# Row sums of a batch's first chunk in 64x32 tiles by query halves, and stages in a new order, in a fused attention and MoE kernel

## The chip, the cores and the metric

The kernel runs on one core of a Trainium2 chip. The metric is the time of one execution on the device, in microseconds (us). A core has five engines that run side by side, each through its own instructions in order: TensorE (PE, matrix products, with its weight loads shown apart as PEld), VectorE (DVE), ScalarE (ACT), GpSimd (POOL) and SyncE (SP, which here only issues transfers). Transfers (DMAs) run on 16 DMA engines, fed by the queues of SP, ACT and POOL.

## The reference

Eight batches of twelve heads, 448 positions, head size 64, all fp32:

```python
q_n, k_n = rmsnorm(q, g_q), rmsnorm(k, g_k)
scores = (q_n @ k_n.T) / sqrt(64)
attn = exp(scores - max) / sum(exp(scores - max))
x = (attn @ v), heads side by side        # 3584 tokens x 768
h = x @ w_in                              # 768 -> 2048
g = h + sin(alpha * h)**2 / alpha
out = g @ w_out                           # 2048 -> 768, fp32
```

## The kernel before

**Tiling.** A batch is a stage. Its twelve heads form three chunks (c = 0, 1, 2) of four heads: two heads `pp` lie on partition halves, two heads `hi` beside each other. Scores are computed transposed, with 64 keys on the partitions and 448 queries along the free dimension: `scores` makes one such tile (four 64x64 matmuls into a pair of PSUM banks), and ScalarE's exp (L361) writes it to SBUF as bf16. There are 7 tiles of keys a chunk, 21 a batch. `attend` then accumulates, over the 7 tiles, the values (weights from `vb`) and the sums of the exponentials over the keys (weights are a tile of ones, so that each sum appears on as many PSUM partitions as the weights have columns). ScalarE turns sums into reciprocals as exp(-ln(sum)) (L412, L413); VectorE multiplies the values by them into `xT` (L421), the input of the first product.

Chunk 0 is treated alone ("ones 0", "values 0"), with 64x64 tiles: contraction over 64 keys (row half `pp`), output on the 64 partitions of `hi`, in the bank `pp`. Chunks 1 and 2 go together ("ones 1", "low 1", "high 1") in 64x32 tiles, eight at a time.

**The two products.** `first_product` computes h in 16 blocks of 128 features, 8 pairs of banks, six 128x128 matmuls a block (L449). Its first four blocks take the k tiles in the order 0, 1, 2, 4, 3, 5, all four blocks at each; tiles 0 and 1 come from chunk 0 and use the first 256 rows of `w_in` (pieces W00, W10), tiles 2 and 3 use W01 and W11, 4 and 5 W02 and W12 (first digit: half of the features; second: rows). ScalarE's sine (L427), a square on GpSimd or ScalarE (L430, L432) and VectorE (L435) make g. `second_product` cuts the output into units of 128 tokens by 384 columns, with 64x64 tiles (L528); VectorE copies and adds the two halves (L534, L535) into one of three `osb` buffers, and SP stores it. The last batch's second product uses whole 128x128 tiles (L509).

**Order.** Each engine's order is written out by hand in the strings `STAGE_0` (batch 0), `STAGE_1` (batch 1) and `STAGE_N` (batches 2 to 7). Tokens are read from left to right: `S` a score tile (`S2` with two matmuls on zeros ahead of it), `o`, `v`, `x`, `y`, `z` with a number so many key tiles of ones 0, values 0, ones 1, low 1, high 1; a number n is n steps of the second product of the batch before (eight matmuls each) and `f` a step of the unit after the current one; `q`, `u`, `g`, `r`, `k` are squares, their reduction, the scaling by g, the inverse root and the scaling of a chunk of q and k; `p` transposes a chunk on PE, `t` by DMA; `l` loads a chunk, `V` values, `W` and `O` pieces of `w_in` and `w_out`; `D` is a small GpSimd copy that waits until a chunk has landed, so that loads behind it start later. A dictionary gives tokens that come at points of the first product. The second string of a stage lists which of four PSUM bank pairs each allocation takes, in order. An allocation waits until the readers of the pair before it have finished. The load of a chunk (three `qk` buffers) waits until its buffer has been read.

The changed lines stand in `attend`, in the plan strings and in the call that loads chunk 1.

Of the kernel before, what the change touches and what calls it, by code (L numbers as in the profile page):

```python
# [17 lines left out]
try:  # L18
# [8 lines left out]
ACT = mybir.ActivationFunctionType  # L27
# [3 lines left out]

STAGE_0 = (
    (
        "q000 u000 G q010 q011 u010 q001 u011 r01 u001 r00 g00 q11 q10 g01 k01 D1 k00 V00 L p012 p00 u10 "
        "V01 u11 W12 S2 S q20 r1 u20 g1 k11 l3 q21 k10 S2 l4 S S4 S W01 g2 S1 u21 p1 r2 k20 o7 S1 V02 S "
        "q30 k21 v7 u30 S S4 q31 D2 u31 S S1 W00 p2 r3 S3 g3 S S2 k31 S2 q40 D4 W02 S2 k30 q41 p3 S1 u40 "
        "W10 l5 W11 O01 q51 S x4 u41 y3 q50 S r4 z2 z2 x3 y4 g4 z1 z2 "
    ),
    "30123103213013230120310232103102310231302130213",
    {-1: 'u50 u51 g5', 1: 'k401 O00 l6', 2: 'k411', 3: 'O10', 4: 'k400', 5: 'k410', 7: 'O11', 8: 'p4 V12 l7 V10 V11'},  # L40
)
STAGE_1 = (
    (
        "2 q31 4 q40 S 2 u31 S 1 S 1 S r2 1 f q41 1 f 1 S S 1 f f k21 k20 1 S t2 2 S 2 S 1 u40 u41 1 q30 "
        "g3 S 2 f o2 u30 S r4 f 1 f 1 S 1 f o5 2 f r3 l5 2 f g4 f S 2 S 2 V11 S 1 S 2 k31 v1 k41 k30 k40 "
        "S v2 S v4 V12 S y1 S y1 S z3 x7 z3 q51 y5 l6 V10 z1 "
    ),
    "0212310313131230222101013032013001230123",
    {-1: 'l7 q50', 0: 'u51', 2: 'g5 t4', 4: 'u50', 8: 't3'},
)  # L50
STAGE_N = (
    (
        "1 r2 q31 q30 f 2 S V10 f 3 V11 f f k20 2 S 3 S 2 k21 S u31 q40 1 t2 1 g3 1 S 1 f u30 S 2 f S f S "
        "r3 q41 f f 1 l5 1 f S 4 u40 S S 5 S S u41 o7 v7 S S 5 S 2 q51 f S 2 S q50 k31 k30 2 S g4 1 u50 S "
        "2 r4 t3 1 S z3 x7 k40 y7 z1 z2 z1 "
    ),
    "01232302102020301301320321310130210231023",
    {-1: 'l6 u51 V12', 1: 'k41', 2: 't4 l7', 3: 'g5'},
)
LAST = "0123012"  # L60

# [7 lines left out]
def kernel(  # L69
# [23 lines left out]
    nc = tc.nc  # L93
    B, H, S, D = q.shape
# [8 lines left out]
    NJ = S // REST  # L103
    assert P == 2 * REST == 2 * D
    NC = NP // 2
# [28 lines left out]
    def bank_pair(name, dtype=F32):  # L134
        slot = int(upcoming.popleft())
        free_at.remove(slot)
        ps = psum.tile([P, 2, 2048 // mybir.dt.size(dtype)], dtype, tag=f"ps{slot}", name=name)
        slot_of[id(ps)] = slot
        return ps

    def give_back(ps):
        free_at.append(slot_of.pop(id(ps)))
# [3 lines left out]
    def strip(c, pp, hi):  # L146

        s = 2 * hi + (pp if c == 1 else 1 - pp)
        return slice(s * 32, s * 32 + 32)

    def load_qk(ci, k_queue=nc.sync):

        b, dp = ci // NC, ci % NC
        qk[ci] = inp.tile([P, 2, 2 * NJ, D], F32, tag="qk", name="qk")
        for which, src, queue in ((0, q, nc.sync), (1, k, k_queue)):
            heads = src[b].rearrange("(dp hi pp) (p j) d -> dp pp p hi (j d)", hi=2, pp=2, j=NJ)[dp]
            rows = qk[ci][:, which].rearrange("p (hi j) d -> p hi (j d)", hi=2)
            if ci == 0:
                continue
            if dp < 2:  # L160
                queue.dma_start(out=rows, in_=heads.rearrange("pp p hi x -> (pp p) hi x"))
            else:
                for pp in range(2):
                    queue.dma_start(out=rows[pp * 64:pp * 64 + 64], in_=heads[1 - pp])
        if ci == 0:
            for hi in range(2):
                for which, src, queue in ((0, q, nc.sync), (1, k, k_queue)):
                    heads = src[b].rearrange("(dp hi pp) (p j) d -> dp hi pp p (j d)", hi=2, pp=2, j=NJ)[dp, hi]
                    rows = qk[ci][:, which].rearrange("p (hi j) d -> p hi (j d)", hi=2)
                    queue.dma_start(out=rows[:, hi], in_=heads.rearrange("pp p x -> (pp p) x"))  # L170
                if hi == 0:
                    load_g()
# [17 lines left out]
    def load_g():  # L190
        for i, (src, queue) in enumerate(((g_q, nc.sync), (g_k, nc.scalar))):
            queue.dma_start(out=g_rows[:, i], in_=src.rearrange("(a d) -> a d", a=1))

    load_qk(0, nc.scalar)
    load_qk(1, nc.scalar)
    load_qk(2)
    nc.gpsimd.dma_start(out=small, in_=moe_alpha.rearrange("(mt p) -> mt p", p=P))
    nc.scalar.preload_act_table_set(EXP_LN)
# [2 lines left out]
    ones = const.tile([P, D], BF16)  # L201
# [58 lines left out]
    qkT, expT, xT = {}, {}, {}  # L260
# [125 lines left out]
    def attend(b, what, tiles=range(NJ)):  # L386

        kind, both = what.split()  # L390
        both = both == "1"
        if tiles[0] == 0:
            avs[what] = bank_pair("av")
        av = avs[what]
        pre = presums.get(b) if what == "ones 0" else None
        last = 1 if pre else NJ - 1
        for j in tiles:
            for hi in range(2):
                for c in ((1, 2) if both else (0,)):
                    for pp in range(2):  # L400
                        r = slice(pp * 64, pp * 64 + 64)
                        o, k = (strip(c, pp, hi), c - 1) if both else (slice(hi * 64, hi * 64 + 64), pp)
                        d = slice(kind == "high", D, 2) if both and kind != "ones" else slice(D // 2 if both else D)
                        w = ones[r, d] if kind == "ones" else vb[b][r, 2 * c + hi, j, d]
                        x = pre.parts[j] if pre else expT[b * NC + c, j]
                        nc.tensor.matmul(av[o, k, :S], w, x[r, hi, :], start=(j == 0), stop=(j == last))  # L406
        if tiles[-1] < last:
            return
        if kind == "ones":
            rec = recs[both] = pre.t if pre else rpool.tile([P, 2, S], F32, tag="rec", name="rec")  # L410
            for k in ((0, 1), (1, 2)) if both and b == 0 else ((0, 2),):
                nc.scalar.activation(rec[:, slice(*k)], av[:, slice(*k), :S], ACT.Ln)  # L412
                nc.scalar.activation(rec[:, slice(*k)], rec[:, slice(*k)], ACT.Exp, scale=-1.0)  # L413
            give_back(avs.pop(what))
        else:
            if b not in xT:
                xT[b] = xpool.tile([P, KT, S], BF16, tag="xT", name="xT")
            first = 0 if not both else 2 if kind == "low" else 3
            for k in (slice(0, 1), slice(1, 2)) if both and b == 0 else (slice(0, 2),):
                kts = slice(first + k.start * (1 + both), first + (k.stop - 1) * (1 + both) + 1, 1 + both)  # L420
                nc.vector.tensor_mul(xT[b][:, kts, :], av[:, k, :S], recs[both][:, k])  # L421
            give_back(avs.pop(what))
# [185 lines left out]
    for b in range(B):  # L608
        plan, slots, h_plan = (STAGE_0, STAGE_1, STAGE_N)[min(b, 2)]
        if b:  # L610
            nc.scalar.preload_act_table_set(EXP_LN)
            fillers.extendleft(reversed(second_product(b - 1)))
        tiles = deque((b * NC + c, j) for c in range(NC) for j in range(NJ))
        upcoming.extend(slots)
        done = {what: 0 for what in STEPS}
        for x in tokens_of(plan):
            if x in "Ff":
                fill(x == "f")
            elif x[0] == "S":
                scores(*tiles.popleft(), int(x[1:] or 0))  # L620
            elif x[0] in STEPS:
                n = int(x[1:] or 1)
                attend(b, STEPS[x[0]], range(done[x[0]], done[x[0]] + n))
                done[x[0]] += n
            else:
                step(b, x)
        first_product(b, {i: [lambda t=t: step(b, t) for t in tasks.split()] for i, tasks in h_plan.items()})
        assert not upcoming and not tiles
# [32 lines left out]
```

## Time and profile before

The median of three runs is 416.54 us (416.4 to 418.31). The profiled execution took 419.68 us, of which the profile's span is 417.9 us.

| engine | busy us | share of the span |
|---|---|---|
| PE | 397.1 | 95% |
| ACT | 317.4 | 76% |
| POOL | 285.3 | 68% |
| DVE | 227.1 | 54% |

"Busy" is the time in which an engine had at least one instruction at work; matmuls overlap on PE, so a busy PE needn't be at its peak. A group of instructions is named by its line, its engine and its operands as out<-in. The chain of waits follows the last instruction back to what released each step, and so shows which engine or transfer sets the end. `x` and a number count instructions. Lines of DMA in it give the start and the time from issue to landing.

### The profile page before, as it was taken

The numbers are of one execution on the slowest core, as the hardware profiler recorded it, in microseconds if no ns is written. First come the engines' busy times: TensorE is split into PE (matmuls) and PEld (weight loads), VectorE is DVE, ScalarE is ACT, GpSimd is POOL, SyncE is SP. The second block draws the span as 40 slices with busy tenths as digits, with TensorE's granted clock in tenths as the row PEclk, the third lists the DMA queues.
The fourth block names the chain that finished last, engine by engine and source line by source line (L and its number), as shares of the span: only waits on it lengthen the run. The fifth ranks groups of instructions, "written<-read, shape, count | busy, mean of one in ns | idle before, by whom it ended". The sixth has DMA issues, their size and how long they took to land.

```text
span 417.9 us, 14897 instructions
## 1 busy us (share of the span) xinstructions
PE 397.1 (95%) x6598; PEld 238.2 (57%) x6601; DVE 227.1 (54%) x339; ACT 317.4 (76%) x467; POOL 285.3 (68%) x270
## 2 busy tenths in 40 slices
PE   2797999889999999999999999999999999999996
PEld 2243558645666557655666456655576556665563
DVE  5786475426674565564575466655565464335511
ACT  4897789748889679877889688987889688886600
POOL 4999889966786879597796688597795784003300
PEclk9999999999999999999999999999999999999999
DMA  8999999798085744847374744736385521620022
GB/s 244 212 220 255 167 218 156 168 284 105 3 164 131 168 139 83 175 92 156 101 175 119 174 134 80 176 81 164 104 131 158 93 46 27 96 61 0 2 75 75
DMA packets 66788, 54.51 MB, mean 130 GB/s; under 512 B 38164, under 2 KB 62500, under 8 KB 66724
## 3 DMA queue, kind: packets, MB, share of 16 engines
q1 hardware_dynamic: 53250, 40.06, 37.8%
q0 software_dynamic: 12512, 11.81, 19.7%
q10 hardware_dynamic: 962, 1.70, 1.1%
q8 instruction: 51, 0.84, 0.8%
q14 instruction: 13, 0.11, 0.1%
HBM read 45.62 MB, written 11.01 MB: 136 GB/s over the span
## 4 chain that ended last, share of the span: by engine, by line
PE 86%; DMA 6%; POOL 4%; issue 2%; DVE 1%; ACTq 0%; SPq 0%; ACT 0%; DVEq 0%; POOLq 0%
PE hps L449 34%; PE ops L528 29%; PE av L406 11%; PE sc L358 6%; PE ops L509 5%; DMA w_in<-in_moe_w_in_dram 3%; DMA qk<-in_k_dram 2%; POOL sq L283 1%; DMA out_dram<-osb 1%; POOL qk L288 1%; POOL vb L182 0%; POOL vb L185 0%; SPq L499 0%; POOL w_in L244 0%; DVE osb L534 0%
## 5 line engine op out<-in xcount | busy, mean ns | idle before, releaser
L361 ACT ACTIVATE expT<-sc 128x896 bf16<-128x896 f32 x168 | 144.9, 914 | 16.9 <-PE sc L358 16.0
L449 PE MATMUL hps<-xT,w_in 128*128 128x448 bf16 x768 | 146.8, 353 | 2.1 <-DMA w_in<-in_moe_w_in_dram 2.1
L528 PE MATMUL ops<-w_out_sb,g_sb 64*64 64x384 bf16 x3072 | 145.6, 323 | 0.2 <-ACT expT L361 0.2
L435 DVE SCALAR_TENSOR_TENSOR g_sb<-s,inv_alpha_sb,hps 128x448 bf16<-128x448 f32 x128 | 80.8, 677 | 67.3 <-POOL s L430 66.9
L449 PEld LDWEIGHTS <-w_in 128*128 128x128 bf16 x768 | 74.4, 98 | 74.0 <-issue 3.0
L528 PEld LDWEIGHTS <-g_sb 64*64 64x64 bf16 x3072 | 91.3, 107 | 38.0 <-issue 2.7
L430 POOL TENSOR_TENSOR s<-s 128x448 f32<-128x448 f32 x64 | 59.5, 932 | 74.7 <-ACT s L427 50.2
L427 ACT ACTIVATE s<-hps,alpha_sb 128x448 f32<-128x448 f32 x128 | 74.4, 626 | 43.2 <-PE hps L449 40.4
L283 POOL TENSOR_TENSOR sq<-qk 128x896 f32<-128x896 f32 x44 | 73.3, 1682 | 26.1 <-DMA qk<-in_k_dram 21.1
L311 POOL TENSOR_TENSOR qkn<-qk,inv 128x448 bf16<-128x448 f32 x80 | 72.7, 938 | 2.5 <-ACT inv L302 2.0
L358 PE MATMUL sc<-qkT 64*64 64x448 bf16 x672 | 58.3, 356 | 3.6 <-DVE qkT L343 2.1
L534 DVE COPY osb<-ops 128x384 f32<-128x384 f32 x48 | 26.7, 557 | 51.3 <-PE ops L528 46.1
L288 POOL TENSOR_TENSOR qk<-qk,gg 128x896 f32<-128x896 f32 (+1 forms) x25 | 50.3, 2016 | 1.2 <-ACT g_sb L280 1.1
L292 DVE TENSOR_REDUCE ms<-sq 128x14 f32<-128x896 f32 x44 | 46.7, 1078 | 6.4 <-POOL sq L283 6.3
L421 DVE TENSOR_TENSOR xT<-av,rec 128x896 bf16<-128x896 f32 (+1 forms) x26 | 25.6, 1015 | 37.2 <-ACT rec L413 30.7
L406 PE MATMUL av<-expT,vb 64*32 64x448 bf16 (+1 forms) x1120 | 37.9, 350 | 2.7 <-issue 2.0
L432 ACT ACTIVATE s<-s 128x448 f32<-128x448 f32 x64 | 36.9, 577 | 3.0 <-DVE g_sb L435 0.2
L358 PEld LDWEIGHTS <-qkT 64*64 64x64 bf16 x672 | 20.7, 107 | 17.3 <-issue 7.9
L406 PEld LDWEIGHTS <-vb 64*32 64x32 bf16 (+1 forms) x1120 | 19.5, 95 | 16.7 <-issue 6.8
L535 DVE TENSOR_TENSOR osb<-osb,ops 128x384 f32<-128x384 f32 x48 | 26.6, 554 | 1.7
L406 PE MATMUL av<-expT,ones 64*32 64x448 bf16 (+1 forms) x672 | 24.5, 349 | 0.0
L509 PE MATMUL ops<-w_out_sb,g_sb 128*128 128x384 bf16 x128 | 21.0, 326 | 0.0
(46 smaller groups left out, 173.5 us busy)
## 6 DMA issues: line engine op xcount, KB each, us to landing
out_dram<-osb SPq DMA_DIRECT2D x39, 192.0 KB, 3.7
qk<-in_q_dram SPq DMA_DIRECT2D x15, 448.0 KB, 5.5
qk<-in_k_dram SPq DMA_DIRECT2D x14, 448.0 KB, 6.3
qk<-in_q_dram SPq DMA_DIRECT2D x18, 224.0 KB, 4.3
qk<-in_k_dram SPq DMA_DIRECT2D x16, 224.0 KB, 4.7
vb<-in_v_dram POOLq DMA_DIRECT2D x16, 224.0 KB, 4.4
w_out_sb<-in_moe_w_out_dram POOLq DMA_DIRECT2D x4, 768.0 KB, 7.7
out_dram<-osb SPq DMA_DIRECT2D x26, 96.0 KB, 3.4
```

The costliest lines, as they stand in the source:

```text
L283: nc.gpsimd.tensor_mul(st.sq[w], qk[ci][:, w], qk[ci][:, w])
L288: nc.gpsimd.tensor_mul(x, x, gg.to_broadcast([P, len(heads) * NJ, D]))
L292: nc.vector.reduce_sum(st.ms[:, w, rows], st.sq[w][:, rows], axis=AX.X)
L311: eng.tensor_mul(n[:, :, hi, :], x[:, hi], inv[:, hi].unsqueeze(2).to_broadcast([P, NJ, D]))
L358: nc.tensor.matmul(sc[pp * 64:pp * 64 + 64, hi, :S], qkt[r, 1, j * REST:(j + 1) * REST], qkt[r, 0, :], start=True, stop=True)
L361: nc.scalar.activation(expT[c, j], sc[:, :, :S], ACT.Exp, scale=SCALE)
L406: nc.tensor.matmul(av[o, k, :S], w, x[r, hi, :], start=(j == 0), stop=(j == last))
L427: nc.scalar.activation(s1, hps, ACT.Sin, scale=alpha_sb[:, m, :])
L430: nc.gpsimd.tensor_mul(s2, s1, s1)
L435: nc.vector.scalar_tensor_tensor(g_sb[:, m, (b % 2) * S:(b % 2 + 1) * S], s2, inv_alpha_sb[:, m, :], hps, op0=ALU.mult, op1=ALU.add)
L449: nc.tensor.matmul(ps[:, m % 2, :S], w_in_sb[m * 2 // MT][:, kt, m % (MT // 2) * P:(m % (MT // 2) + 1) * P], x[:, kt, :], start=(kt == ORD ...
L528: nc.tensor.matmul(st["ps"][os, r, :HALF], g_sb[rs, m, c0 + o * 64:c0 + o * 64 + 64], w_out_sb[rs, m, half * HALF:(half + 1) * HALF], star ...
```

## The change

In batches 1 to 7 the sums of chunk 0 are made in 64x32 tiles: each of the four (pp, hi) sums is split into the two halves `qh` of the queries, and each half gets its own strip of 32 PSUM partitions, so that eight matmuls of 224 columns take the place of four of 448. A strip then holds the sums of one half of the queries only. ScalarE makes the reciprocals of both strips in three instructions (one Ln, two Exp, 448 elements each), and four VectorE copies bring each half's reciprocals to the other strip of its pair, so that the multiply finds them on all 64 partitions. Batch 0 keeps the sums as they were.

All three plans are new: the order of tokens, the bank pairs and the tokens beside the first product. Chunk 1's k is loaded from SP's queue and not from ACT's.

```diff
     load_qk(0, nc.scalar)
-    load_qk(1, nc.scalar)
+    load_qk(1)
     load_qk(2)
...
         last = 1 if pre else NJ - 1
+        halved = what == "ones 0" and b > 0
         for j in tiles:
+            if halved:
+                for hi in range(2):
+                    for qh in range(2):
+                        for pp in range(2):
+                            r, o = slice(pp * 64, pp * 64 + 64), slice((2 * hi + qh) * 32, (2 * hi + qh) * 32 + 32)
+                            nc.tensor.matmul(av[o, pp, :S // 2], ones[r, :D // 2], expT[b * NC, j][r, hi, qh * S // 2:(qh + 1) * S // 2],
+                                             start=(j == 0), stop=(j == NJ - 1))
+                continue
...
             rec = recs[both] = pre.t if pre else rpool.tile([P, 2, S], F32, tag="rec", name="rec")
-            for k in ((0, 1), (1, 2)) if both and b == 0 else ((0, 2),):
+            if halved:
+                cols = [slice(0, S // 2), slice(S // 2, S)]
+                nc.scalar.activation(rec[:, :, cols[0]], av[:, :, cols[0]], ACT.Ln)
+                nc.scalar.activation(rec[:, :, cols[1]], rec[:, :, cols[0]], ACT.Exp, scale=-1.0)
+                nc.scalar.activation(rec[:, :, cols[0]], rec[:, :, cols[0]], ACT.Exp, scale=-1.0)
+                for hi in range(2):
+                    for qh in range(2):
+                        src, dst = (slice((2 * hi + x) * 32, (2 * hi + x) * 32 + 32) for x in (qh, 1 - qh))
+                        nc.vector.tensor_copy(rec[dst, :, cols[qh]], rec[src, :, cols[qh]])
+            for k in () if halved else ((0, 1), (1, 2)) if both and b == 0 else ((0, 2),):
                 nc.scalar.activation(rec[:, slice(*k)], av[:, slice(*k), :S], ACT.Ln)
                 nc.scalar.activation(rec[:, slice(*k)], rec[:, slice(*k)], ACT.Exp, scale=-1.0)
```

The plans, cut to what the prediction speaks of:

```diff
 STAGE_0 = (
     (
-        "... D1 k00 V00 L p012 p00 u10 V01 u11 W12 S2 ... W01 g2 ... V02 ... D2 ... W00 ... D4 W02 ... W10 l5 W11 O01 ..."
+        "... D1 k01 k00 V02 W00 p012 q11 g1 W02 ... q21 ... q20 ... V00 g2 ... W11 q30 ... q31 ... V01 S D2 g3 k31 W01 l5 o3 W10 o3 D4 W12 ..."
...
 STAGE_1 = (
     (
-        "2 q31 4 q40 S ... k21 k20 1 S t2 2 S ... o2 ... o5 ... v1 ... v2 S v4 V12 S y1 S y1 S z3 x7 z3 q51 y5 l6 V10 z1 "
+        "1 q31 2 S 2 q30 ... k20 f k21 f S t2 f 1 S ... u40 o6 V12 o1 v1 2 S 2 f r3 v4 S v2 1 k31 f S f S 1 S f 1 S 1 k30 1 t3 S q50 2 S S z4 l6 S r4 x5 x1 z1 x1 y6 V11 y1 z1 z1 g5 k41 k40 "
...
 STAGE_N = (
     (
-        "1 r2 q31 q30 f 2 S V10 ... S S 5 S S u41 o7 v7 S S 5 S 2 ... 2 r4 t3 1 S z3 x7 k40 y7 z1 z2 z1 "
+        "f q40 f 1 f 2 q41 1 S 1 r2 5 f S f f S 2 S 1 u40 k20 1 k21 S 1 u41 1 S 2 S 1 q31 1 o7 1 f f 1 S t2 f 1 r4 S 2 f 1 l5 q30 S 3 S 1 u31 1 S 2 u30 g3 V10 S 2 S S k41 3 S v6 r3 k30 S k31 v1 S 2 V12 g4 2 S 2 S 2 q51 l6 S t3 z3 x7 y5 y2 z4 V11 "
-    "01232302102020301301320321310130210231023",
+    "01223131310312323203013012301021310231023",
-    {-1: 'l6 u51 V12', 1: 'k41', 2: 't4 l7', 3: 'g5'},
+    {-1: 'k40', 0: 't4', 2: 'q50', 3: 'u50', 4: 'u51 g5', 6: 'l7'},
```

## The prediction

> **What bounds the kernel.** I read the page's busy shares first (PE 95%), then busy time in windows cut where each batch's first product starts and, for the first three, ends.
>
> ```profile
> core 0: us, PE busy (x) PEld busy (x) DVE busy (x) ACT busy (x) POOL busy (x), PEclk, DMA share, GB/s
> 0.00:41.79 41.79, 28.99 (x459) 13.83 (x462) 29.62 (x51) 30.87 (x48) 34.86 (x41) 1.00 1.01 233
> ...
> 57.85:90.20 32.35, 28.76 (x721) 21.34 (x722) 14.92 (x24) 27.44 (x36) 31.01 (x30) 1.00 0.88 194
> ...
> 137.50:184.81 47.31, 47.31 (x855) 28.83 (x854) 27.09 (x40) 39.07 (x58) 37.35 (x34) 1.00 0.58 136
> ```
>
> A steady stage (47.31 us) is all PE: 47.31 busy, at full clock, with the others at 39, 37 and 27. Stage 1's attention (57.85 to 90.20) has 3.6 us without PE. Stage 0 is bound elsewhere: DMA is at its limit (share 1.01), and the chain of waits runs through one weight load:
>
> ```profile
> 30.60 11.14 DMA w_in<-in_moe_w_in_dram
> 41.74 0.05 issue
> 41.79 16.06 PE hps L449 x84
> ```
>
> PE had started that product at 37.20, did 12 matmuls and stood 2.1 us. The waits inside 57.85 to 90.20 name stage 1's loss:
>
> ```profile
> DVE osb L534 <- DMA out_dram<-osb: 5.1, 2, 3.9
> ...
> PE av L406 <- issue: 1.6, 1, 1.6
> ...
> PE sc L358 <- DVE osb L535: 1.4, 1, 1.4
> ...
> PE av L406 <- DVE osb L535: 0.4, 1, 0.4
> ```
>
> Stores stand on SP's queue behind a transpose that waits for GpSimd; VectorE's copies wait for the stores' buffers (three), and PE twice for a bank (1.8 us). The 1.6 us has no visible cause.
>
> Last, PE in order of time in a steady stage:
>
> ```profile
> 171.18 1.49 PE L406 MATMUL av<-expT,ones 64*64 64x448 bf16 x28
> 172.51 1.49 PE L406 MATMUL av<-expT,vb 64*64 64x448 bf16 x28
> ...
> 180.36 0.36 PE L358 MATMUL sc<-qkT 64*64 64x448 bf16 x4
> 180.65 0.76 PE L406 MATMUL av<-expT,vb 64*32 64x448 bf16 x24
> 181.22 1.51 PE L406 MATMUL av<-expT,ones 64*32 64x448 bf16 x56
> 182.55 2.27 PE L406 MATMUL av<-expT,vb 64*32 64x448 bf16 x88
> 184.75 18.33 PE L449 MATMUL hps<-xT,w_in 128*128 128x448 bf16 x96
> ```
>
> Seven groups of four 64x64 matmuls take 1.33 us (171.18 to 172.51); so do seven groups of eight 64x32 matmuls (181.22 to 182.55). Both are 0.19 us a group: eight run side by side as readily as four, and columns set the time. From 180.36 to 180.65 one group costs 0.29: a change of tile shape adds 0.10.
>
> [...]single records here start 3 to 4 ns apart, eight within 24. [...]
>
> **The change, part by part.** *Sums.* Per batch, 7 groups of four 448-column matmuls become 7 groups of eight of 224: 7 x (0.189 - (224/2.4 + 2.3 = 0.0957)) = 0.65 us less on PE. The 28 added matmuls, each with its weight load, are inside that figure if loads keep up[...]. I take 0.096, since 64x32 loads start 3 to 4 ns apart in the trace and none delays a group.
>
> *Tile changes.* The sums used to sit between 64x64 work. Now they are entered and left once in stages 2 to 7: +0.10 + 0.12 = 0.22 us. Counting changes along the plans, stage 1 has seven before and seven after (it loses two detours at its end), so 0.
>
> *ScalarE.* Before 0.92 + 0.95 = 1.87 us (Ln, Exp, 896 elements). After Ln 0.534 and two Exp of 0.577, the 448-element rows of batch 0: 1.69. It has 8 us of slack a stage: 0.
>
> *Copies.* Four per stage, fp32, SBUF to SBUF, 448 elements, 32 partitions; no row before shows one. [...]So 1.6 to 2.5 us a stage, on an engine idle for 20. What can suffer is what queues behind them. Running sum of a steady stage from its start (a fill of eight matmuls 0.325, a score group 0.19, an exp 0.83 to 0.91, first exp at 3.1 behind the table load as before): seventh score at 9.0, its exp ends at 10.4, the sums reach their seventh group at 10.55 (0.15 to spare) and end at 10.65. Ln and Exps fill 10.9 to 12.6, copies 12.6 to 14.2. The unit of the second product that ends at 14.4 needs copy and add, 1.15 us, and its bank is next taken by the twelfth score at 16.4: 0.8 us to spare. The values' multiply comes ten scores after the sums, at 21.4. Continued to the 21st score (24.3, exp ends 25.9), with the last sums' seventh group at 26.3, the sum finds no place where PE waits. Cost 0; with copies of 0.63, still 0.
>
> So stages 2 to 7: 6 x (-0.65 + 0.22) = -2.6 us. Stage 1's own: -0.65.
>
> *Stage 1's order.* The units end at the same fill counts or later: the fifth now has the sums and values ahead of it, about 19.5 us after the stage's first fill (78.2) instead of 75.7, when VectorE began to wait. The transpose still stands ahead of stores two and three, and still waits for GpSimd's squares and scalings (8.4 us), but one weight load and one V load less lie ahead of those (1.7 us), so about 70.2 for 71.66. Store two then goes at 73.7 and lands, at the 4.4 us that it took before (75.19 to 79.6), at 78.1. The copies' wait goes: -1.8. Bounds: 0 if GpSimd is no earlier, -3.4 if the unexplained gap goes too.
>
> *Stage 0's order.* The first product waits for its last weight piece: W02 before, W01 now. GpSimd's queue from the gate at 10.44: gate 0.18, V02 1.26, W00 1.26, scaling 2.1, W02 0.74, two squares 3.36, V00 0.75, scaling 2.1, W11 0.74, two squares 3.36, V01 0.75, gate 0.2, scaling 2.1: sum 18.9, so W01 is issued at 29.4, not 30.60. The same three V and three weight pieces stand ahead of it, and DMA is saturated, so it lands 11.1 (as W02) to 9.9 us (median of the row) later: 40.5 to 39.3. Needed after 8 matmuls instead of 12, it leaves 88 x 0.19 = 16.8 us: the product ends at 56.1 to 57.3 against 57.85. I take -1.1. Bounds: -2.3 (no stall: 38.7 + 16.8) and +0.2 (the row's slowest landing, 11.8). Chunk 1's k, moved from ACT's to SP's queue behind its q, goes ahead of chunk 2 there; ScalarE's first exp comes 0.7 us sooner by my sum, but later it waits for the squares, so 0.
>
> Sum: -1.1 - 0.65 - 1.8 - 2.6 = -6.2 us. The profiled span 417.9 becomes 411.7. That execution took 419.68, 1.8 around the span; the median is 416.54. The difference carries over: 410.3.
>
> **Rivals.** *B, only PE's share is real*: stages 0 and 1 stall as before. For it: DMA there is saturated and the order of loads only redistributes it. Against: W01 is issued earlier. -3.3 us: 413.2.
>
> *C, the sums don't get shorter*: groups of eight at 224 columns still take 0.19 to 0.20, because loads or starts limit them; then only tile changes remain (+1.3 to +1.8) beside the orders' -2.9: 415.2. For it: nothing traced runs so short. Against: the 3 to 4 ns spacing.
>
> *D, slower*: VectorE, held in order behind the four copies that wait for ScalarE, returns the bank of that second-product unit late, and PE waits at the twelfth score, every stage. It starts to bite when a copy takes over 0.64 us (0.8 + 0.2 us of slack over four), and 0.1 more on each costs 0.4 x 7 = 2.8 us. To end 0.5% above before, it must undo 6.2 + 2.1 us, 1.19 a stage: copies of 0.94. At 1.0: 6.2 undone by 10.1, so 420.4. For it: copies across partition strips appear nowhere in the trace. Against: twice the dearest estimate.
>
> **How the numbers follow.** The forecast has 0.55, B 0.21, C 0.10, D 0.08; 0.06 for stage 0 or 1 losing what the rest gains (about 416). The forecast's own range, from the bounds, is 407.5 to 413.5. For 8 in 10 I take 407.5 to 415: it leaves out D and half of C. About 0.5% (2.1 us) is what a measurement of this kernel can tell from none: faster is the forecast and B, 0.76; same takes C and the last case, 0.15; slower 0.09.
>
> **What would show it.** Right: sums as 56 matmuls in about 0.67 us; steady stages of 46.9 us with PE busy throughout; copies near 0.39 us; first product of batch 0 ended by 57; stage 1 without waits for stores. Wrong: PE waiting on VectorE's osb steps in every stage (D), 1.3 us for the sums (C), or W01 landing after 41.

## The result and the profile after

The changed kernel takes 439.85 us (median of four runs, 438.12 to 441.54) against 416.94 for the kernel before beside it. The ratio is 1.0544, with an interval of 1.0494 to 1.0594: 5% slower, where 410.3 had been forecast. The profiled execution took 440.3 us, of which the span is 438.5.

The windows are cut as in the prediction: to the start of batch 0's first product, then batch 1's attention, then stages from one first product's start to the next (stages 3 and 7).

```profile
core 0: us, PE busy (x) PEld busy (x) DVE busy (x) ACT busy (x) POOL busy (x), PEclk, DMA share, GB/s
0.00:40.04 40.04, 29.99 (x448) 13.54 (x451) 25.91 (x46) 28.90 (x44) 33.95 (x40) 1.00 1.01 241
58.30:90.97 32.67, 29.19 (x750) 19.75 (x750) 20.50 (x27) 25.71 (x36) 29.07 (x26) 0.95 0.77 155
...
140.97:192.27 51.30, 48.39 (x881) 30.20 (x882) 32.27 (x44) 39.00 (x59) 37.09 (x34) 0.97 0.61 124
...
348.57:395.48 46.91, 46.91 (x882) 28.54 (x882) 24.49 (x40) 38.06 (x55) 18.57 (x18) 1.00 0.37 67
```

Stage 3 has 2.9 us without PE, and a clock of 0.97. Stage 7 is what had been predicted for every stage: 46.91 us, all of it PE, at full clock. What differs in it is GpSimd: 18.57 us busy instead of 37.09, because there is no further batch to prepare. VectorE differs as well: 24.49 busy instead of 32.27, although its work is nearly the same.

The waits name the place, and the costliest groups name an operation that takes three times what had been estimated (0.39 us):

```profile
PE sc L358 <- DVE osb L553: 14.5, 5, 2.9
...
PE sc L358 <- DVE xT L439: 3.5, 1, 3.5
```

```profile
L428 DVE COPY rec<-rec 32x448 f32<-32x448 f32 x28 | 34.3, 1225 | 9.4 <-ACT rec L424 9.1
```

Five waits of 2.9 us at a score, one in each of stages 2 to 6, and one of 3.5 in stage 1. Now stage 3 in order of time, PE first:

```profile
169.06 0.86 PE L404 MATMUL av<-expT,ones 64*32 64x224 bf16 x56
169.86 1.50 PE L546 MATMUL ops<-w_out_sb,g_sb 64*64 64x384 bf16 x32
...
174.87 0.82 PE L546 MATMUL ops<-w_out_sb,g_sb 64*64 64x384 bf16 x16
178.59 0.59 PE L358 MATMUL sc<-qkT 64*64 64x448 bf16 x4 [2.91 <-DVE osb L553]
178.92 1.54 PE L546 MATMUL ops<-w_out_sb,g_sb 64*64 64x384 bf16 x16
```

The 56 small matmuls of the sums are over in 0.80 us (169.06 to 169.86). The score at 178.59 is the twelfth of its stage, and waits 2.91 us for a bank that VectorE empties. Behind it the same 16 matmuls take 1.54 us instead of 0.82. VectorE and GpSimd at that time:

```profile
171.80 5.56 DVE L428 COPY rec<-rec 32x448 f32<-32x448 f32 x4 [1.26 <-ACT rec L424]
177.39 0.56 DVE L552 COPY osb<-ops 128x384 f32<-128x384 f32 x1
```

```profile
171.97 2.16 POOL L288 TENSOR_TENSOR qk<-qk,gg 128x896 f32<-128x896 f32 x1
174.07 0.77 POOL L182 DMA_DIRECT2D vb<-in_v_dram  x1
174.86 1.84 POOL L311 TENSOR_TENSOR qkn<-qk,inv 128x448 bf16<-128x448 f32 x2
```

The four copies take 5.56 us together. Single records show how that divides: 0.383, 2.180, 2.571 and 0.389. The second starts at 172.19, in the middle of GpSimd's scaling by g (171.97 to 174.13), and ends 0.24 after it; the third starts at 174.39, while GpSimd issues its load of V, and ends 0.26 after the two scalings (to 176.70). The first (171.80) began before the scaling by g, the fourth (176.97) after the last scaling. In stage 7 GpSimd has no instruction between 376 and 384 us, and VectorE's four take 1.58:

```profile
379.40 1.58 DVE L428 COPY rec<-rec 32x448 f32<-32x448 f32 x4 [2.30 <-ACT rec L424]
```

By stages, measured between the starts of first products (stage 0 up to the end of its own; e1 and e5 are runs told of below):

| us | before | predicted | after | e1, order alone | e5, copies left out |
|---|---|---|---|---|---|
| stage 0 | 57.85 | 56.75 | 58.30 | 58.63 | 58.64 |
| stage 1, attention | 32.35 | 29.9 | 32.67 | 28.72 | 28.30 |
| stages 2 to 6 | 47.3 to 47.9 | 46.9 | 50.0 to 52.9 | 47.3 to 47.5 | 46.9 to 47.8 |
| stage 7 | 47.31 | 46.9 | 46.91 | 47.31 | 46.9 |
| the rest | 43.0 | 43.0 | 43.0 | 43.0 | 43.0 |

Of the 20.6 us by which the span grew, stages 2 to 6 make 20.2 (257.60 instead of 237.36), stage 0 0.45, stage 1 0.32, and stage 7 gives 0.40 back.

The trace suggests theory L: a VectorE copy from SBUF to SBUF doesn't run beside a GpSimd instruction that works on SBUF. What it shows is the holding, 2.18 and 2.57 us beside GpSimd's work for 0.38 and 0.39 without it; why the one holds the other was not shown. The rivals: theory S, the copies are slow on their own because they cross partition strips; and theory O, the new order is to blame whatever the copies do.

### The profile page after: what moved, and what is told of

Its sections match the earlier page's. It is cut to its first block, busy times and chain, and to the rows that moved or that the text cites. A ratio compares the mean times of both kernels' runs of the same rounds, so it can differ in the third digit from the quotient of the medians.

```text
span 438.5 us, 15331 instructions
## 1 busy us (share of the span) xinstructions
PE 406.5 (93%) x6795; PEld 245.7 (56%) x6797; DVE 260.3 (59%) x367; ACT 317.7 (72%) x474; POOL 287.3 (66%) x270
## 4 chain that ended last, share of the span: by engine, by line
PE 84%; DVE 10%; ACT 3%; DMA 1%; issue 1%; DVEq 0%
PE hps L467 33%; PE ops L546 24%; PE av L415 10%; PE sc L358 8%; DVE rec L428 7%; PE ops L527 5%; PE sc L354 2%; PE av L404 1%; PE tp L336 1%; DMA qk<-in_k_dram 1%; ACT rec L424 1%; ACT rec L423 1%; ACT rec L422 1%; DVE ms L292 1%; DVE osb L552 1%; DVE osb L553 1%
## 5 line engine op out<-in xcount | busy, mean ns | idle before, releaser
L546 PE MATMUL ops<-w_out_sb,g_sb 64*64 64x384 bf16 x3072 | 156.0, 334 | 0.0
L546 PEld LDWEIGHTS <-g_sb 64*64 64x64 bf16 x3072 | 97.1, 111 | 38.8 <-issue 3.2
L358 PE MATMUL sc<-qkT 64*64 64x448 bf16 x672 | 65.5, 382 | 19.6 <-DVE osb L553 14.5
L358 PEld LDWEIGHTS <-qkT 64*64 64x64 bf16 x672 | 23.7, 112 | 35.5 <-issue 28.7
L439 DVE TENSOR_TENSOR xT<-av,rec 128x896 bf16<-128x896 f32 (+1 forms) x26 | 25.7, 1016 | 29.4 <-ACT rec L431 25.8
L428 DVE COPY rec<-rec 32x448 f32<-32x448 f32 x28 | 34.3, 1225 | 9.4 <-ACT rec L424 9.1
L415 PE MATMUL av<-expT,vb 64*32 64x448 bf16 (+1 forms) x1120 | 37.9, 350 | 0.0
L553 DVE TENSOR_TENSOR osb<-osb,ops 128x384 f32<-128x384 f32 x48 | 26.6, 554 | 1.7
L415 PEld LDWEIGHTS <-vb 64*32 64x32 bf16 (+1 forms) x1120 | 20.0, 95 | 12.1 <-issue 2.5
## 6 DMA issues: line engine op xcount, KB each, us to landing
w_out_sb<-in_moe_w_out_dram POOLq DMA_DIRECT2D x4, 768.0 KB, 14.5
```

The lines of the kernel that those rows point to most:

```text
L358: nc.tensor.matmul(sc[pp * 64:pp * 64 + 64, hi, :S], qkt[r, 1, j * REST:(j + 1) * REST], qkt[r, 0, :], start=True, stop=True)
L428: nc.vector.tensor_copy(rec[dst, :, cols[qh]], rec[src, :, cols[qh]])
L546: nc.tensor.matmul(st["ps"][os, r, :HALF], g_sb[rs, m, c0 + o * 64:c0 + o * 64 + 64], w_out_sb[rs, m, half * HALF:(half + 1) * HALF], star ...
```

## The experiments

### The two halves of the change

**e1_order_only** has the changed kernel's plans and the sums of before.

```diff
-        halved = what == "ones 0" and b > 0
+        halved = False
```

> The changed kernel's plans with the sums of before (64x64 tiles, 448 columns, reciprocals on all partitions at once, no copies). Theory L (a copy [...]and GpSimd exclude each other, and VectorE held by it returns a bank late): without the copies nothing stalls, steady stages are PE alone, 46.9 + 0.65 - 0.22 = 47.3 us, and the whole is that of before, 417 +- 2 us. Theory O (the new order itself loses, through GpSimd's 8 us waits for the inverse roots or the bank pairs): steady stages stay near 50 to 52 us, 434 to 440 us. Theory S (copies across strips are slow by themselves) says the same as L here.

415.64 us (20 runs), ratio 0.9952 (0.9934 to 0.9970). The same kernel again, under the label e10_order_again, beside e9 below:

> The new order with the old sums once more, on the chip of the two others: 415 to 416 us, steady stages of 47.3. The difference to the kernel with GpSimd copies from batch 2 is what the sums are worth: 6 x 0.43 = 2.6 us if PE's share is all that counts.

415.56 (8 runs), 0.9956 (0.9927 to 0.9985). The new order alone gains some 2 us; stage 1's attention lasts 28.72 us, and no stage waits at the twelfth score. In e1, stage 1's attention and stage 3 (columns as above):

```profile
58.63:87.35 28.72, 28.43 (x721) 19.20 (x722) 15.36 (x23) 25.61 (x35) 26.70 (x24) 1.00 0.85 170
...
134.66:181.97 47.31, 47.31 (x853) 28.84 (x854) 26.84 (x40) 38.83 (x58) 36.99 (x34) 1.00 0.68 134
```

Theory O falls.

**e2_sums_only** is the reverse: the plans of before, the new sums and copies (the lines of the diff in `attend`, nothing else).

> The plans of before with the new sums and the four copies. In the trace of before GpSimd stands idle for 5 us (171.2 to 176.2 of a steady stage) just where the copies would fall. Theory L: copies of 0.39 us there, no wait, steady stages 46.9, stage 1 nearly as before: 413 to 415 us. Theory S: copies keep their mean of 1.2 us, 4.9 a stage; VectorE has some slack there, so 1 to 3 us a stage are lost: 420 to 435 us.

433.7 us, 1.0390 (1.0308 to 1.0471). In stages 2 to 7 of that order GpSimd is idle at the copies, and all 24 take 0.38 to 0.39 us. Of the 12.3 us by which its span is longer than before, 9.8 lie in batch 1's attention, here in order of time, VectorE and then GpSimd:

```profile
75.14 11.14 DVE L428 COPY rec<-rec 32x448 f32<-32x448 f32 x4 [1.06 <-ACT rec L424]
```

```profile
73.05 4.12 POOL L288 TENSOR_TENSOR qk<-qk,gg 128x896 f32<-128x896 f32 x2
77.11 0.76 POOL L182 DMA_DIRECT2D vb<-in_v_dram  x1
77.89 7.19 POOL L311 TENSOR_TENSOR qkn<-qk,inv 128x448 bf16<-128x448 f32 x8
```

The copies take 2.27, 7.90, 0.54 and 0.39 us: the second, which starts at 77.4, while GpSimd issues a V load, isn't let in between eight scalings that follow each other, and ends 0.25 after the eighth (85.08). PE waits 11.8 us at a score, the first of these two lines:

```profile
PE sc L358 <- DVE osb L553: 11.8, 1, 11.8
...
PE sc L358 <- DVE xT L439: 3.5, 6, 0.6
```

So the same copy takes 0.38 or 7.9 us in one kernel, and what goes with it is GpSimd. Stages 2 to 7 still take 47.8 to 48.2 us, not the 46.9 that theory L expected: the values' multiply stands behind the copies on VectorE, and PE waits 0.6 us a stage for it (the second line); the other 0.3 us stay open. In that order even fast copies cost more than the sums save.

### The copies elsewhere, or otherwise

**e4_psum_copies** lets the copies read PSUM instead of SBUF, with the same shapes, strips and place. ScalarE writes the reciprocals once more, into the sums' bank, for them to read.

```diff
+                nc.scalar.activation(av[:, :, cols[1]], rec[:, :, cols[0]], ACT.Exp, scale=-1.0)
...
-                        nc.vector.tensor_copy(rec[dst, :, cols[qh]], rec[src, :, cols[qh]])
+                        nc.vector.tensor_copy(rec[dst, :, cols[qh]], av[src, :, cols[1]])
```

> The changed kernel with the same four copies at the same place, but reading the reciprocals from PSUM (one more Exp on ScalarE writes them into the sums' own bank). Theory L: [...]GpSimd does not hold it: 0.62 us each[...], flat, though GpSimd works beside it; VectorE is held 2.5 us after the Exps, and the twelfth score may wait up to 0.5 us: 413 to 418 us. Theory S: 1.2 us or more each, 435 us or more.

All 28 copies take 0.61 to 0.63 us, in stage 3 under the same GpSimd work (VectorE, then GpSimd, in order of time):

```profile
173.33 2.52 DVE L429 COPY rec<-av 32x448 f32<-32x448 f32 x4 [1.73 <-ACT rec L425]
```

```profile
173.03 2.07 POOL L288 TENSOR_TENSOR qk<-qk,gg 128x896 f32<-128x896 f32 x1
...
175.83 1.84 POOL L311 TENSOR_TENSOR qkn<-qk,inv 128x448 bf16<-128x448 f32 x2
```

They cross strips as before and are not held up, and in e2 copies that cross strips took 0.38 us: theory S falls. The whole is no faster, 443.38 us (1.0601, 1.0540 to 1.0661). The sums' bank is now held until the last copy has read it, and the score that wants it waits 2.7 us in six stages (`PE sc L358 <- DVE rec L429: 16.4, 6, 2.7`). One stall went and another came, of the same size.

**e3_late_copies** issues the four copies just ahead of the values' first tile, some seven us later.

```diff
+        if what == "values 0" and b > 0 and tiles[0] == 0:
+            rec, cols = recs[False], [slice(0, S // 2), slice(S // 2, S)]
+            for hi in range(2):
+                for qh in range(2):
+                    src, dst = (slice((2 * hi + x) * 32, (2 * hi + x) * 32 + 32) for x in (qh, 1 - qh))
+                    nc.vector.tensor_copy(rec[dst, :, cols[qh]], rec[src, :, cols[qh]])
...
-                for hi in range(2):
-                    for qh in range(2):
-                        src, dst = (slice((2 * hi + x) * 32, (2 * hi + x) * 32 + 32) for x in (qh, 1 - qh))
-                        nc.vector.tensor_copy(rec[dst, :, cols[qh]], rec[src, :, cols[qh]])
```

> The changed kernel with the four copies issued later on VectorE, just ahead of the values' first tile, nothing else moved. GpSimd is idle then (176.7 to 185.1 of the changed kernel's steady stage). Theory L: copies of 0.39 us, steady stages 46.9 with PE busy throughout, stage 1 shorter by 3 us or more: 411 to 416 us. Theory S: copies of 1.2 us still, and VectorE held for 4.9 us at another place: 425 us or more. Theory O: 430 us or more.

427.38 us, 1.0218 (1.0157 to 1.0279). In stages 2 to 6 the copies take 0.38, 0.38, 0.39 and 1.03 (the last behind a scaling); batch 1's meet GpSimd at work as before (1.92 to 1.03 us). The wait at the twelfth score is gone; the values' multiply, queued behind the copies, now returns its bank late: `PE sc L358 <- DVE xT L441` has 11.9 us in seven waits, about 1.5 in a steady stage, which lasts 48.6 to 49.4. More than half of the loss is gone, the rest has a new name.

**e7_scalar_copies** gives the copies to ScalarE.

```diff
-                        nc.vector.tensor_copy(rec[dst, :, cols[qh]], rec[src, :, cols[qh]])
+                        nc.scalar.copy(rec[dst, :, cols[qh]], rec[src, :, cols[qh]])
```

> The changed kernel with the four copies on ScalarE, at the same place. [...]0.58 us each whatever GpSimd does; but the next exps stand 2.3 us behind them. By the running sum of the prediction the tenth score waits for the eighth exp's bank for about 1.4 us in each stage: 416 to 424 us. If copies across strips are slow on any engine, or if the delay of the sums' consumers is what costs, 430 us or more.

428.2 us, 1.0248 (1.0189 to 1.0308), above what was expected. Each copy takes 0.562 us under the same GpSimd work, so ScalarE isn't held by it. But 2.25 us on ScalarE stand ahead of the exps, and the list of waits shows PE behind them:

```profile
PE sc L358 <- ACT expT L361: 11.4, 8, 2.3
```

A stage takes 49.0 us. The slack that ScalarE has over a stage (8 us) isn't at this place.

**e6_gpsimd_copies** gives them to GpSimd (`nc.gpsimd.tensor_copy`).

> The changed kernel with the four copies on GpSimd in place of VectorE, at the same place of the program. If VectorE's position in line was the cost (held behind Exps and GpSimd, then late with a bank), it is gone: GpSimd has 8 us idle in a steady stage, and its copies can't wait for itself. 4 copies of 0.6 to 1 us, hidden: 411 to 415 us, faster than both kernels. If it is GpSimd's time or what queues behind it there (squares, scalings, the inverse roots) that matters, 2 to 4 us a stage are lost again: 425 to 440 us.

422.35 us, 1.0102 (1.0047 to 1.0156), between the two expectations, at 0.55 us a copy. Stages 2 and 7 last 46.90 us. In batch 1 the copies queue behind the scaling by g and a V load, and PE waits 4.3 us. Stages 3 to 6 last 47.8 to 49.5; part of that is gaps without a visible cause (`PE av L415 <- issue`, 3.9 us in three). The latter stays open.

**e9_gpsimd_from_2** therefore keeps the old sums in batch 1 as well.

```diff
-        halved = what == "ones 0" and b > 0
+        halved = what == "ones 0" and b > 1
...
-                        nc.vector.tensor_copy(rec[dst, :, cols[qh]], rec[src, :, cols[qh]])
+                        nc.gpsimd.tensor_copy(rec[dst, :, cols[qh]], rec[src, :, cols[qh]])
```

> The kernel with GpSimd copies, but with the new sums in batches 2 to 7 only; batch 1 has the old sums. If batch 1's 4.3 us wait (copies behind a V load and two scalings on GpSimd) was all that the GpSimd copies cost, it is gone, and what remains is the new order and 6 x 0.43 us: 413 us (412 to 416), faster than before and than the order alone. If GpSimd's copies cost in each stage, 417 us or more.

415.72 us (16 runs), 0.9964 (0.9939 to 0.9988), and e10 beside it 0.9956: no difference between them. From the first product of batch 1 to that of batch 7, e9 takes 283.4 us and e10 284.3, so of the 2.4 us that six stages should give, 1 is seen in the profiles and none in the medians.

**e5_no_copies** leaves the four copies out.

> The changed kernel without the four copies; half of chunk 0's reciprocals are then those of other queries, so the values of chunk 0 are scaled wrongly. The rest of the work and its order are unchanged. If the copies carry the whole loss, this is the order alone less what the sums save: 415.6 - 0.65 - 6 x 0.43 = 412.4 us (411 to 414), with steady stages of 46.9. If the sums or their three ScalarE instructions cost by themselves, it stays at 420 us or more.

413.77 us (20 runs), 0.9915 (0.9894 to 0.9935). It is faster than the kernel before, so the copies carry the whole loss. Without them the sums bring 1.5 us over the order alone (the ratios' quotient, 0.9963 of 416). Stages 2, 6 and 7 last 46.9 us, the others 47.5 to 47.8.

### The copies in place, GpSimd elsewhere

The last three leave the VectorE copies where they are and move GpSimd's work. **e8_moved_gpsimd** puts the V load behind, and the scaling by g after the seventh values tile in the plan:

```diff
-... S 2 u30 g3 V10 S 2 S S k41 3 S v6 r3 k30 S k31 v1 ...
+... S 2 u30 S 2 S S 3 S v6 r3 g3 k41 k30 S k31 V10 v1 ...
```

> The changed kernel; in the plan of batches 2 to 7 alone GpSimd's scaling, V load and two scalings that fall on the copies (g3, V10, k41) are issued later, behind the inverse roots. Copies, sums and their places stay. Theory L: the copies of batches 2 to 6 meet an idle GpSimd, 0.39 us each, and those stages fall from 51.5 to about 46.9 us; batch 1's copies still wait: 439.85 - 5 x 4.6 = 417 us (414 to 421). If holding VectorE behind ScalarE's three instructions is enough to lose the bank, or if GpSimd's later work then comes late for the next stage, stages stay at 49 us or more: 428 us or more.

434.09 us, 1.0390 (1.0364 to 1.0416): not what was expected, because the edit didn't do what it was for. The plan sets GpSimd's order, not its times; nothing ahead of the scaling waited for anything, so it ran at 171.81 as ever. Only the V load moved. The copies took 4.67 instead of 5.56 us and PE's wait fell from 2.9 to 2.0 (`PE sc L358 <- DVE osb L553: 10.1, 5, 2.0`): the size of the wait follows that of the copies.

**e11_idle_gpsimd** makes GpSimd wait. The scaling that stands first in its queue needs inverse roots, which come later.

```diff
-... S 2 u30 g3 V10 S 2 S S k41 3 S v6 r3 k30 S k31 v1 S 2 V12 ...
+... S 2 u30 S 2 S S 3 S v6 S r3 k31 g3 k30 v1 S V10 2 k41 V12 ...
```

> The changed kernel with the four VectorE copies where they are, but GpSimd kept waiting while they run, in the stages from 2 on: one chunk's scaling, which waits for inverse roots that ScalarE makes after the copies' exponentials, is now first on GpSimd's queue (k31, one score later), with the scaling by g, the other scaling and the V load behind it. TensorE's and VectorE's orders are untouched, and no work is left out. Theory L (a copy from SBUF to SBUF cannot run beside a GpSimd instruction that reads and writes SBUF): copies 0.38 to 0.39 us each in stages 2 to 7, no wait of PE for the osb steps there, stages of 46.9 to 47.3 us; batch 1 keeps its slow copies (stage 1 near the changed kernel's 32.7); whole time 416 to 419. Theory S (copies that cross strips are slow on their own in a busy kernel, whatever GpSimd does): copies stay above 1 us, stages 50 or more, whole time 434 to 440.

**e12_idle_from_2** is the same with the old sums in batch 1.

> As e11_idle_gpsimd, and the new sums only in batches 2 to 7, so that batch 1 has no copies. Theory L: every copy at 0.38 to 0.39 us; stage 1 as in e1_order_only (28.7 us), stages 2 to 7 of 46.9 to 47.3; whole time 413 to 415, 0 to 2.5 us under e1_order_only. Theory S: 428 or more.

They took 438.53 us (1.0526, 1.0474 to 1.0578) and 435.59 (1.0443, 1.0402 to 1.0484). Both totals miss what theory L expected by 20 us; what it says of the copies' own times holds. In e12 every copy takes 0.380 to 0.390 us, in e11 every one of stages 2 to 7. VectorE and GpSimd in stage 3 of e12:

```profile
169.75 1.58 DVE L428 COPY rec<-rec 32x448 f32<-32x448 f32 x4 [1.26 <-ACT rec L424]
```

```profile
166.52 3.32 POOL L283 TENSOR_TENSOR sq<-qk 128x896 f32<-128x896 f32 x2 [0.73 <-DVE ms L292]
179.70 1.83 POOL L311 TENSOR_TENSOR qkn<-qk,inv 128x448 bf16<-128x448 f32 x2 [9.86 <-ACT inv L302]
```

Stage 4 of e12, cut into attention and first product:

```profile
208.45:237.02 28.57, 28.57 (x785) 19.29 (x785) 16.35 (x28) 25.71 (x37) 17.10 (x15) 1.00 0.46 100
237.02:259.68 22.66, 19.86 (x108) 9.76 (x104) 11.97 (x17) 13.19 (x22) 19.79 (x19) 0.92 0.82 153
```

The attention lasts 28.57 us in each of stages 2 to 7, all of it PE, against 28.98 in the kernel before: 0.41 gained, 0.43 predicted. The first product, always 18.33 before, now takes 22.7. GpSimd, which had waited 9.86 us where the copies needed 1.5, is late with the scalings, and with its share of the squares in the first product behind them. PE in order of time in stage 2's:

```profile
146.50 10.70 PE L467 MATMUL hps<-xT,w_in 128*128 128x448 bf16 x48 [2.79 <-DVE g_sb L453]
```

There are five such waits (14.0 us), each followed by a slow stretch (48 matmuls in 10.70 us instead of 9.26). The inverse roots that GpSimd waits for came 8 us later than meant: I had placed the wait on `r3`, counting from the roots that the trace shows at 172.5, and these were those of another chunk. A wait just long enough was not tried.

## Why the prediction was wrong

**Sums: right.** Seven groups of eight at 224 columns: 0.096 us a group was predicted, single records show 0.0960. The 224/2.4 + 2.3 ns behind it agrees with the records of before: 128x128 matmuls of 448 columns mostly start 189 to 190 ns apart, those of 384 columns 162 to 163, so 64 columns are some 27 ns, or 2.4 columns a ns. The change of tile shape ahead costs 0.10 (0.10 predicted); the 56 matmuls and the way back take 0.80 together, of which the way back is 0.11 (0.12 predicted; 0.13 in the trace of before, between 83.13 and 83.45). The whole, -0.43 a stage, is what e12's attentions show (-0.41). Rival C is out.

**ScalarE: right.** Ln 0.545, Exps 0.577 each, no wait for them.

**Copies: this step failed.** The 0.39 and 0.63 us were my estimates, which nothing in the trace of before showed: the nearest there, from PSUM with 384 elements, took 0.557. The 0.39 was right for the instruction (0.380 to 0.390 where GpSimd is idle), and from PSUM it took 0.61 to 0.63 (e4). "On an engine idle for 20" and "Cost 0" were wrong: I priced the copies by VectorE's own occupation and never laid GpSimd's row beside them, although the new plan puts the scaling by g, a V load and two scalings exactly there. In place of 1.56 us they take 5.56 in each of stages 2 to 6. The running sum had 0.8 us to spare for the bank of the unit behind them, at the twelfth score, and it is at the twelfth score that PE stands.

**Rival D happened**, at its place: VectorE held behind the copies, one bank late, every stage with a GpSimd that works. Even its price fits: copies over 0.64 us each, 2.56 together, begin to bite; 5.56 - 2.56 is 3.0, and the wait is 2.9. Its reason was wrong. It asked whether crossing strips is slow, which it isn't (0.38 us in e2), and so its chance was set by "twice the dearest estimate" of a copy that runs alone. The point from which it decides had been put at 0.94 us a copy in seven stages; the mean is 1.225, with one stage of seven at 0.38.

**What the stall cost beyond itself.** Not in the prediction at all: stages 2 to 6 lose 23.0 us against 46.91 each, of which the waits are 14.5. The other 8.5 is TensorE at half its clock: windows cut at 177.85 and 181.26, in stage 3, have a clock of 0.50, as have 6.83 us of stage 4 and 3.41 each of stages 5 and 6. That is 17.06 us in all, and half of it is the 8.5. The durations agree (16 matmuls in 1.54 us behind the wait of stage 3, 0.82 ahead of it). In stage 2 the same wait of 2.9 us brought no drop (50.00 us); in stages 3 to 6 it did.

The clock records of the fourteen traces suggest why. In each trace all changes of the clock lie whole multiples of 3.413 us apart (in the one of after: 82.27, 85.69, 177.85, 181.26 and so on, to 437.26). Cut into such pieces, the traces have 45 pieces at full clock with 2.0 us or more without PE, and 44 of them are followed by half the clock; of the 1574 pieces with less, none is. In the traces of before and after alone it is 7 of 7, with 2.07 to 2.90 us without PE, and none of 225, with up to 1.94. Stage 2's wait is cut into 0.96 and 1.94 us, stage 3's into 2.16 and 0.75. This is a count, and no experiment moved a wait to try it.

**Stage 1's order: right in direction, undersized.** -1.8 was predicted for the waits, with a bound of -3.4. The order alone brings -3.6 (28.72 for 32.35), since the gap of 1.6 us without visible cause went as well. In the changed kernel copies of 1.93, 1.14, 1.03 and 1.03 us hand all of it back: the chain of waits runs through them, PE waits 3.5 us for `DVE xT L439`, and 3.41 us at half the clock follow (from 82.27).

**Stage 0's order: the step was right, its sum wrong.** In the changed kernel W01 goes out at 27.8 us and lands at 36.7 (29.4, and 39.3 to 40.5, were predicted), and PE no longer stands for a piece of weights. The term that failed is PE's own arrival at the product: the prediction kept the 37.20 of before (its 38.7 is that and eight matmuls), and it was 40.04. So the product ends at 58.30, not at 56.75. Two lines of PE in order of time, of before and then of after, show why:

```profile
18.79 0.89 PE L336 MATMUL tp<-ident,qkn 64*128 64x64 bf16 x28
```

```profile
18.56 1.46 PE L336 MATMUL tp<-ident,qkn 64*128 64x64 bf16 x28
```

The same 28 transposes take 0.89 or 1.46 us: in the kernel after, TensorE is still at a low rate at 18.6 us, and until about 24 (four matmuls of a score take 0.59 us there, 0.38 later). The first clock record of a trace, 1.00, begins where the durations have fallen to those of the full rate (in the kernel after, single matmuls of a score take 0.58 us at 20.9, 0.53 at 23.9 and 0.37 at 24.9): at 24.25 us in the kernel after and at 16.75 before. Of twelve profiles with the new plan, one (e10) has it at 18.25; its first product starts at 37.7 and ends at 55.98, 1.9 us earlier than before. The others have it at 22.0 to 25.1, and the product starts at 39.1 to 40.5. Both profiles with the old plan have it by 17. In the profiles, then, what the step saves is there with the early full rate and is gone with the late one.

Why the full rate comes late stays open. How busy PE is from 14 to 18 us doesn't decide it alone: that is 3.4 us of 4 after and 3.8 and 4.0 in the two with the old plan, but 3.3 in e10. And e1 is the same program as e10; PE works in both without a pause from 15.1 to 18.2 us, and e1 has the full rate at 25.1.

**The forecast without its wrong step.** e5, which has everything but the copies, takes 413.77, not 410.3: stage 0 gives +0.8 instead of -1.1, stage 1 gives -4.1 instead of -2.5, and the sums' 0.43 a stage is partly lost in stages 3 to 5 to small gaps whose cause stays open.

## What to carry to other kernels

Before an instruction is given to an idle VectorE, look at what GpSimd does in the same microseconds, and at whether the operands lie in SBUF: 0.38 us became 2.6 and, in e2, 7.9, while copies from PSUM stayed at 0.61 to 0.63 (e4). When a wait is moved away, follow the bank or queue that it lets through: four cures here (another source, another place, another engine, another order of GpSimd) each removed that wait and found another, of 1.4 to 2.8 us a stage. And a saving of 0.4 us a stage, a hundredth, did not pay here for a helper operation on a second engine, on none of the three engines tried; the order of stage 1 (-3.6 us), not the sums, holds most of what there was to gain.

## What the runs showed of the hardware beyond expectation

- A VectorE copy that had been held by a GpSimd instruction on tensors ended 0.24 to 0.26 us after that instruction did (44 copies, 13 of them in the kernel after), one held by the issue of a V load 0.19 to 0.22 us after it (5 copies, one of them in the kernel after, 0.215).
- It was sometimes let in between GpSimd instructions that follow each other, and sometimes not: 1.03 us behind one of several scalings (batch 1) and behind the first of two (e8), 2.57 behind both (stages 2 to 6), 7.90 behind eight (e2). The copies that were not let in had started while GpSimd was issuing a V load, but so had one in batch 1 that was let in (1.14 us). What decides it stays open.
- The hold is mutual in part: two scalings between which copies were let in took 2.12 us (e8), otherwise 1.84.
- A copy of 448 fp32 elements on 32 partitions to another strip takes 0.38 us from SBUF and 0.62 from PSUM on VectorE, 0.56 on ScalarE and 0.55 on GpSimd.
- The clock column of the windows stayed at 1.00 in stage 0 while the transposes' and scores' own durations show a low rate; there, the durations have to be read. The records behind the column begin at 24.25 us.
